# A fused linear-attention and feed-forward kernel: loads and output transfers moved to the SP queue, with a new order of the work

## The chip, the cores and the metric

The kernel runs on 1 core of one Trainium2 chip. The metric is the device time of the whole launch in microseconds (us), as the median of several runs. The engines are PE (TensorE, matrix products), DVE (VectorE), ACT (ScalarE), POOL (GpSimd) and SP (SyncE, which here only issues DMA transfers). Each runs its own list of instructions in order; a semaphore tells one engine that another, or a transfer, is done.

## What is computed

First a linear attention with a decaying state, for 4 sequences of 768 steps, 8 heads of 48 numbers. Then every one of the 3072 tokens (384 numbers) passes a feed-forward layer of 2048 hidden numbers whose activation is a rational function:

```python
for t in range(S):
    cur = np.einsum('bhd,bhe->bhde', u[None] * kt, vt)
    y[:, :, t] = np.einsum('bhd,bhde->bhe', rt, state + cur)
    state = w[None, :, :, None] * state + np.einsum('bhd,bhe->bhde', kt, vt)
...
h = x @ w_in
P = a[0] + a[1] * h + a[2] * h2 + a[3] * h3
Q = 1.0 + np.abs(b[0]) * np.abs(h) + np.abs(b[1]) * h2
g = P / (Q + 1e-06)
return (g @ w_out).astype(np.float32)
```

The weights w_in and w_out come as 8-byte numbers, and the kernel turns them into pairs of 4-byte ones itself.

## The kernel before

The attention is cut into 24 blocks of 128 steps (four sequences of six, `blk`), and two blocks make one tile of 256 tokens, 12 in all. The hidden numbers are worked in slices: a slice is one tile and up to four groups of 128 hidden numbers (the table `SL`, 50 slices, the first 47 of four groups).

- **A block** loads r, k and v (`att_load`, L445, three transfers of 192 KB: `rh`, `kn`, `vn`) and a copy of v with its halves exchanged (`att_v`, as a transfer L455 or as a copy L400). POOL scales k and makes the bonus term, PE transposes k and r (L494), forms the scores and the state (`akv`, L516 and L520) and the result (`y`, L564 and L566); DVE masks, adds and moves (L485, L507, L527, L541, L545, L577 or L580). PE turns the result (`x`, L590) and it is split into a high and a low part, `xthi` and `xtlo` (L400, L604).
- **A piece of weights** (28 of them, `swi` and `swo`) is loaded (`cv_load`, L370), handled by ACT (L375, L378), by DVE (L382, L385, with one of the PSUM buffers `pa0`, `pa1`, `h0`, `h1` in between), by POOL (L389), then split by ACT (L394) and POOL (L397).
- **A slice** is PE's first product (L615, 36 matmuls, into one of the two PSUM buffers `h0` and `h1`), then ACT: absolute value (L652), square (L661), square (L656), logarithm (L665), exponential (L669); DVE: L673, L678, L682, L686 and L691. The L691 is the last that reads the buffer `h`, so the slice after the next can begin its first product behind it. Then PE's second product (L619 to L621), and the result goes out by ACT or DVE (L738 to L742) and an output transfer of 192 KB (`put_dma`, L746).
- **A check of the inputs** (`pro_flag`, L327 to L344, some 15 tiny DVE instructions) runs once, somewhere among the weights.

Which engine does each step, in which order and in which buffer, stands in the string `ORDER`: a table of some 1,770 entries that a planner wrote. `Lk.5Slx2` is the load of k of block 5, issued by SP into buffer `lx2`; the capital letter is the engine (D, A, G, P, S for DVE, ACT, POOL, PE, SP). `cl` is the load of a piece of weights, `Lr`, `Lk`, `Lv`, `LV` are loads of a block, `od` is an output transfer, `f1` and `f2` are the two products, `ex` is L669, `lo` is L691, `warm` are matmuls on ones whose result is not used. The loop that reads the table:

```python
for task in ORDER.split():
    task, e, slot = re.fullmatch(r"(.+)([A-Z])((?:[a-z]+\d)*)", task).groups()
    name, *at_ = task.split(".")
    at_ = [int(x) for x in at_]
    here[:] = re.findall(r"[a-z]+\d", slot)
    FN[name](ENG[e], *at_)
```

A transfer waits, on the engine that issues it, for the readers of the buffer that it fills, and for an earlier transfer that used the same one of eight semaphores (`DMAHW0` to `DMAHW7` in the lists below). Nothing behind it on that engine starts before.

Of the kernel before, what the change touches and what calls it, by code (L numbers as in the profile page):

```python
# [49 lines left out]
pad.2G plGos0 pad.0G mskG Lr.0A warm.1P tr.0Ph0 wS Lr.1A pad.1G warm.3P tr.1Ppa0 cl_D ctrA pow.0D pow.2D inv.2Dta0 coefS betaA rxD  # L50
bet2A inv.3D inv.0D warm.4P turn.0.1Ph1 pow.1D pow.3D turn.2.1P turn.3.1P inv.1D warm.2P turn.1.1P cl.1S c0.1A Lk.0Slx0 ba.0Gm0
tre.0D tre.1D c2.1Dh0 sqD tab.1A sk.0G Lk.1Slx1 sk.1G Lv.0Sldv0 uwS warm.7P tk.0Ppa1 Lv.1Sldv1 tke.0A warm.3P akv.0Ppa0pa1 kvm.0A
LV.0.0Avx0 c3.1D ae.0.1.0D w128D ae.0.0.0D ae.0.1.1D bb.0G bs.0Ddt0 ae.0.0.1D Lk.2Slx2 tk.1Ph1 tke.1A warm.3P akv.1Ph0 cu.1A
LV.1.0Avx1 LV.0.1A warm.1P y.0Ph1 ae.1.0.0D kvx.0D cl.2S cu.2A c0.2A cl.0S c0.0A ba.1Gm1 bb.1G bs.1Ddt1 ae.1.1.0D c2.2Dpa0
ae.1.0.1D bv.0G sk.2G warm.3P tk.2Ppa1 tke.2A cr.1Gta1 c3.2D ye.0D Lr.2S warm.3P tr.2Ppa0 bv.1G ba.2Gm2 cr.2Gta2 c2.0Dpa1 kvm.1A
kvx.1D ae.1.1.1D LV.1.1A cl.8S c0.8A ch.1A warm.5P y.1Ph1 tre.2D c3.0D c2.8Dpa0 ye.1D bb.2G c3.8D Lv.2Sldv2 akv.2Ph0 ae.2.1.0D
cu.0A co.1G warm.1P x.0Ph1 cl.4S c0.4A c2.4Dpa1 bs.2Ddt0 xh.0Axt0 x.1Ppa0 xh.1A xl.0D cu.4A cr.0Gta3 ch.0A kvm.2A c3.4D xl.1D
Lr.3S Lk.3Slx0 warm.5P tr.3Ph1 tre.3D sk.3G tk.3Ppa1 ae.2.0.0D kvx.2D ae.2.0.1D ae.2.1.1D Lv.3Sldv3 ch.2A LV.3.0Avx2 tke.3A
LV.2.0Avx0 LV.2.1A LV.3.1A warm.3P akv.3Ppa0pa1 ae.3.1.0D ae.3.1.1D cl.9S c0.9A c2.9Dh1 kvm.3A kvx.3D c3.9D ae.3.0.0D ae.3.0.1D
co.0G co.2G f1.0.0Ph0 f1.0.1P f1.0.2P cl.6S Lk.4Slx1 c0.6A cu.9A cu.6A ba.3Gm3 bb.3G sk.4G bv.2G cl.5S c0.5A c2.6Dpa1 c2.5Dpa0  # L60
cu.5A cu.8A tk.4Ph1 tke.4A cl.3S c0.3A f1.0.3P z.0Ata4 c3.6D bs.3Ddt1 bv.3G c3.5D c2.3Dpa1 cr.5Gta5 y.2Ph1 ye.2D c3.3D cl.21S
# [4 lines left out]
cr.4Gta0 co.5G ca.2G c0.22A cu.12A ch.6A co.6G c0.13A cu.18A c0.12A ch.8A bs.4Ddt0 d.0D c2.7Dpa1 lo.0Dta5 c2.22Dpa0 c3.7D c3.22D
LV.4.1A ch.4A c2.12Dpa1 warm.19P f1.1.0Ph1 f1.1.1P f1.1.2P f1.1.3P z.1Ata4 warm.3P tk.5Ph0 tke.5A c0.16A c2.16Dpa0 ca.1G co.8G
bv.4G co.4G cr.7Gta3 c3.12D warm.3P tr.5Ph0 tre.5D c3.16D c2.13Dpa1 cu.21A cu.22A t.1Ata6 u3.1D f2.0.0P os.0.0Aos1 akv.5Ph0
ae.5.1.0D c3.13D ae.5.1.1D kvm.5D ae.5.0.0D kvx.5D ae.5.0.1D warm.2P f2.0.1P Lk.7Slx0 LV.5.1S cr.12Gta1 cr.11Gta0 ba.5Gm1 ch.11A
co.11G bb.5G bs.5Ddt1 cu.13A LV.11.0Avx2 Lr.6A cl.19S ch.12A q.1A ln.1A cl.25A y.4Ppa0pa1 ye.4D Lk.6Alx1 cl.15S Lr.7A cl.17S  # L70
cl.24S c0.10A c2.10Dpa0 warm.6P y.5Ph0 bv.5G ye.5D ex.1A hi.1Dta0 cr.21Gta2 sk.7G cr.9Gta5 warm.2P x.4Ppa1 xh.4Axt2 c0.19A warm.8P
x.5Ph0 xh.5A xl.5D xl.4D warm.26P f1.2.0Ph0 f1.2.1P f1.2.2P ch.21A cu.10A os.0.1Aos2 co.21G co.12G c0.25A cu.15A cr.13Gta2 ch.7A
cl.20A ch.9A co.9G ca.3G co.7G ch.13A c0.15A cl.14S f1.2.3P t.2Ata1 Lk.8Slx2 ba.6Gm2 co.13G bb.6G p.1D d.1D c2.19Dpa1 lo.1Dta4
c3.10D f2.1.0P f1.3.0Ph1 f1.3.1P f1.3.2P f1.3.3P flagD c2.15Dpa0 z.2Ata6 q.2A u3.2D ln.2A ex.2A cl.26S cu.16A c0.14A os.1.0Aos3
Lv.9Aldv3 z.3Ata5 t.3Ata3 q.3A cl.23A c3.15D c3.19D c2.25Dpa0 bs.6Ddt0 c3.25D hi.2Dta2 p.2D d.2D lo.2Dta6 u3.3D sk.6G tk.6Ppa1
f2.1.1P ba.7Gm3 ca.5G bb.7G cr.10Gta0 ch.10A tr.6Ppa0 tre.6D cr.22Gta4 ch.22A c0.20A c2.14Dpa0 bs.7Ddt1 c3.14D ln.3A ex.3A
hi.3Dta1 p.3D d.3D lo.3Dta5 Lv.7Sldv4 Lk.9Slx1 LV.7.0Svx1 LV.7.1S LV.6.0Svx0 c0.26A c0.23A cl.27S LV.6.1S co.10G ca.4G co.22G
# [843 lines left out]
```

## Time and profile before

| | |
|---|---|
| median of 3 runs | 552.5 us (551.88 to 552.65) |
| the profiled execution | 552.59 us |
| its span, first to last instruction | 550.9 us |
| PE busy | 522.2 us (95%) |
| DVE busy | 479.2 us (87%) |
| ACT busy | 349.3 us (63%) |
| POOL busy | 150.6 us (27%) |
| mean granted TensorE clock | 0.986 |
| read from memory, written | 27.87 MB, 4.72 MB |

A share of busy time is a mean over stages with different limits, so the stretches below are read one by one. "Idle before <-releaser" in a row is the time that the engine stood before the instruction, and what it waited for. A busy PE also holds the `warm` matmuls.

### The profile page before, as it was taken

To read this page: it belongs to the slowest core of one execution; us is meant where nothing else is said; L and a number is where in the kernel's file an instruction comes from. 1 tells how busy PE (TensorE), PEld (TensorE's weight loads), DVE (VectorE), ACT (ScalarE), POOL (GpSimd) and SP (SyncE) were. 2 spreads that over 40 slices of the span, in tenths; PEclk is the share of its full clock that TensorE was granted. 3 is DMA by queue.
4 is the path that set the end of the run, shared out by engine and by line. 5 is a ranking of instruction groups with operands and counts; after the bars stand their busy time and mean duration, and the time that the engine had idled before them with its cause. 6 is when DMAs were issued, how large, how long until landed. Compare 5 with 4: busy or idle time off the path is not lost.

```text
span 550.9 us, 14335 instructions
## 1 busy us (share of the span) xinstructions
PE 522.2 (95%) x6213; PEld 493.6 (90%) x6213; DVE 479.2 (87%) x648; ACT 349.3 (63%) x428; POOL 150.6 (27%) x167
## 2 busy tenths in 40 slices
PE   7895995999999999999999999999999999999994
...
DVE  6996999999899998988989988899698898887774
...
GB/s 160 247 288 285 152 120 107 33 16 29 68 15 2 2 56 76 21 59 52 40 46 80 61 61 30 1 30 23 41 34 15 15 15 2 31 15 15 1 29 65
DMA packets 88455, 33.60 MB, mean 61 GB/s; under 512 B 81600, under 2 KB 84800, under 8 KB 88384
## 3 DMA queue, kind: packets, MB, share of 16 engines
q1 hardware_dynamic: 60288, 21.13, 16.1%
...
q14 instruction: 20, 0.16, 0.1%
HBM read 27.87 MB, written 4.72 MB: 59 GB/s over the span
## 4 chain that ended last, share of the span: by engine, by line
PE 63%; DVE 9%; ACT 3%; issue 1%; ACTq 0%
PE h L615 27%; PE o L619 9%; PE o L621 9%; PE o L620 9%; PE akv L516 2%; DVE h L686 2%; DVE q L682 1%; DVE h L673 1%; PE y L566 1%; PE tk L494 1%; PE akv L520 1%; PE tr L494 1%; DVE g L678 1%; PE y L564 1%; PE x L590 1%
## 5 line engine op out<-in xcount | busy, mean ns | idle before, releaser
L615 PE MATMUL h<-xthi,wi 128*128 128x256 f32 x1152 | 220.7, 285 | 9.4 <-DVE sc L527 6.1
L615 PEld LDWEIGHTS h<-xthi,wi 128*128 128x128 f32 x1152 | 182.2, 189 | 12.7 <-ACT wo L394 6.6
L615 PE MATMUL h<-xtlo,wi 128*128 128x256 f32 x576 | 161.6, 281 | 0.1
L619 PE MATMUL o<-wo,g 128*128 128x384 f32 x384 | 133.0, 346 | 0.1
L620 PE MATMUL o<-wo,g 128*128 128x384 f32 x384 | 129.9, 338 | 0.0
L621 PE MATMUL o<-wo,l 128*128 128x384 f32 x380 | 128.7, 339 | 0.1
L615 PEld LDWEIGHTS h<-xtlo,wi 128*128 128x128 f32 x576 | 109.2, 190 | 0.2 <-DVE xtlo L604 0.2
L661 ACT ACTIVATE z<-h,off,root 128x1024 f32<-128x1024 f32 (+1 forms) x48 | 57.4, 1196 | 60.1 <-PE h L615 52.3
L678 DVE SCALAR_TENSOR_TENSOR g<-h,sig,z 128x1024 fp32r<-128x1024 f32 (+1 forms) x48 | 61.0, 1271 | 37.2 <-ACT z L669 37.0
L652 ACT ACTIVATE q<-h 128x1024 f32<-128x1024 f32 (+2 forms) x50 | 49.3, 987 | 45.2 <-PE h L615 40.0
L665 ACT ACTIVATE z<-q,sig 128x1024 f32<-128x1024 f32 (+1 forms) x48 | 54.9, 1143 | 36.4 <-DVE h L673 33.7
L619 PEld LDWEIGHTS o<-wo,g 128*128 128x128 f32 x384 | 72.8, 190 | 1.4 <-PE idle_bank L779 0.6
L620 PEld LDWEIGHTS o<-wo,g 128*128 128x128 f32 x384 | 72.8, 190 | 0.0
L621 PEld LDWEIGHTS o<-wo,l 128*128 128x128 f32 x380 | 72.0, 189 | 0.6 <-DVE l L691 0.5
L475 POOL TENSOR_TENSOR m<-rh,kn 128x384 f32<-128x384 f32 x23 | 25.5, 1108 | 162.5 <-PE x L590 67.9
L682 DVE SCALAR_TENSOR_TENSOR q<-q,sig,g 128x1024 f32<-128x1024 f32 (+2 forms) x50 | 64.7, 1294 | 1.7
L673 DVE SCALAR_TENSOR_TENSOR h<-z,sig,h 128x1024 f32<-128x1024 f32 (+1 forms) x48 | 61.1, 1272 | 4.3 <-ACT q L652 2.7
L686 DVE SCALAR_TENSOR_TENSOR h<-h,sig,q 128x1024 f32<-128x1024 f32 (+2 forms) x50 | 62.3, 1246 | 1.0
L656 ACT ACTIVATE q<-q,off,root 128x1024 f32<-128x1024 f32 (+2 forms) x50 | 60.4, 1209 | 0.8
L691 DVE TENSOR_TENSOR l<-h,z 128x1024 fp32r<-128x1024 f32 (+1 forms) x48 | 58.1, 1211 | 2.0
L669 ACT ACTIVATE z<-z 128x1024 f32<-128x1024 f32 (+1 forms) x48 | 50.5, 1052 | 6.6 <-DMA rh<-in_r_dram 5.2
L527 DVE TENSOR_TENSOR sc<-akv,mask 64x256 f32<-64x256 f32 x96 | 40.3, 420 | 6.1 <-PE akv L520 2.8
...
## 6 DMA issues: line engine op xcount, KB each, us to landing
...
out_dram<-os ACTq DMA_DIRECT2D x24, 192.0 KB, 2.0
vn<-in_v_dram SPq DMA_DIRECT2D x19, 192.0 KB, 4.5
kn<-in_k_dram SPq DMA_DIRECT2D x18, 192.0 KB, 3.6
rh<-in_r_dram ACTq DMA_DIRECT2D x12, 192.0 KB, 2.8
rh<-in_r_dram SPq DMA_DIRECT2D x12, 192.0 KB, 3.8
...
```

Of the source, the lines that this page charges most:

```text
L615: nc.tensor.matmul(o, wi_of(j, cc, part), x_[:, cc], start=(n == 0), stop=(n == 3 * NCC - 1))
L619: nc.tensor.matmul(o, hi, wo_of(j, HI), start=first, stop=False)
L620: nc.tensor.matmul(o, hi, wo_of(j, LO), start=False, stop=False)
L621: nc.tensor.matmul(o, lo, wo_of(j, HI), start=False, stop=last)
L656: nc.scalar.activation(g["q"], g["q"], AF.Square, scale=RB, bias=KB)
L661: nc.scalar.activation(g["t"], g["h"], AF.Square, scale=RA, bias=KA)
L665: nc.scalar.activation(g["z"], g["q"], AF.Ln, bias=QE)
L673: nc.vector.scalar_tensor_tensor(g["h"], g["t"], KAP, g["h"], op0=ALU.add, op1=ALU.mult)
L678: nc.vector.scalar_tensor_tensor(g["hi"], g["h"], c0, g["z"], op0=ALU.add, op1=ALU.mult)
L682: nc.vector.scalar_tensor_tensor(g["q"], g["q"], qe, g["hi"].bitcast(F32), op0=ALU.add, op1=ALU.mult)
L686: nc.vector.scalar_tensor_tensor(g["h"], g["h"], c0, g["q"], op0=ALU.add, op1=ALU.subtract)
L691: nc.vector.tensor_mul(g["lo"], g["h"], g["z"])
```

## The change

Only the string `ORDER` differs. Before, ACT issued 28 loads and all 24 output transfers besides its arithmetic; now it issues the first two loads of r and the last two output transfers, and SP all others. 26 loads and 22 output transfers so move from ACT's list to SP's. The order of all tasks was planned anew, with a planner that counts PE's instruction fetches as longer; a few tasks change engine (three `os` from DVE to ACT, one `xh`, one `tke`, one `sk`, one `ba` and one `bv` to DVE, and the like), and the `warm` matmuls go from 120 to 100. From the diff, two lines of before and two of the change, in which `cl.7A`, `cl.12A`, `cl.12S` and `Lv.5S` can be seen:

```diff
-x.2Ppa0 Lv.4Sldv4 cl.18S q.0A Lk.5Slx2 cl.22S xh.2Axt1 x.3Ppa1 xh.3A xl.2D c0.18A cr.3Gta0 ca.0G akv.4Ph1 ae.4.0.0D cl.7A ln.0A
-cl.12A ex.0A LV.4.0Avx1 xl.3D ae.4.1.0D kvm.4D c2.18Dpa0 ae.4.0.1D ba.4Gm0 cr.8Gta1 bb.4G cl.13S Lv.5Sldv0 Lv.11Sldv1 sk.5G
...
+tre.4D cl.12S c0.12A c2.12Dpa1 warm.1P y.3Ph1 ye.3D z.0Ata3 u3.0D warm.1P x.2Ppa0 xh.2Axt1 q.0A ln.0A c3.12D Lk.5Slx2 Lv.4Sldv4
...
+p.0D c2.16Dpa0 ch.5A bb.4G co.9G bb.5G cr.11Gta4 c0.13A LV.4.0Avx0 cl.22S Lv.5Sldv0 cl.10S cu.10A LV.5.0Avx1 LV.4.1A d.0D warm.1P
...
```

What the lists of the engines say of it, at three places.

**ACT, around the exponential of the first slice** (L669 into `z_769`, now `z_714`; `swi`, `swo` are pieces of weights, a DMA row is a transfer that ACT issues). Before:

```order
L375 ACTIVATE swo_778<-swo_778 128x384 [waits DMAHW7_49]
L370 DMA swi_0_832<-in_moe_w_in_dram 128x1024 [waits DMAHW2_49]
L665 ACTIVATE z_769<-q_678,sig 128x1024 [waits DVE_49,Activation_49]
L370 DMA swo_835<-in_moe_w_out_dram 128x768 [waits DMAHW6_49]
L669 ACTIVATE z_769<-z_769 128x1024 [waits Activation_49]
L400 COPY vx_838<-vn_776 64x192
```

Now:

```order
L656 ACTIVATE q_783<-q_783,off,root 128x1024 [waits Activation_49]
L665 ACTIVATE z_714<-q_783,sig 128x1024 [waits DVE_49,Activation_49]
L400 CAST xthi_791<-x_854 128x3x128 [waits PE_49]
L378 ACTIVATE swi_2_663<-swi_2_663 128x512
L669 ACTIVATE z_714<-z_714 128x1024 [waits Activation_49]
L394 CAST wo_868<-bwo_673 128x384 [waits Pool_49]
```

Two transfers, with their waits for a semaphore, are gone from ahead of the exponential; a copy and a conversion stand there instead.

**DVE, around L691 of the third slice** (`h_1252`, now `h_1249`; the L344 is the last instruction of the check of the inputs). Before:

```order
L344 TENSOR_REDUCE oks<-okw 128x1
L382 TENSOR_SCALAR c_1394<-swi_1_1142 128x512
L673 SCALAR_TENSOR_TENSOR h_1252<-z_1314,sig,h_1252 128x1024
L385 SCALAR_TENSOR_TENSOR swi_1_1142<-swi_1_1142,c_1394 128x512
L385 SCALAR_TENSOR_TENSOR swo_1096<-swo_1096,c_1324 128x384
L382 TENSOR_SCALAR c_1419<-swo_1102 128x384
L485 TENSOR_REDUCE dt_1421<-m_1318 128x8
L385 SCALAR_TENSOR_TENSOR swo_1102<-swo_1102,c_1419 128x384
L678 SCALAR_TENSOR_TENSOR g_1424<-h_1252,sig,z_1314 128x1024
L682 SCALAR_TENSOR_TENSOR q_1396<-q_1396,sig,g_1424 128x1024
L686 SCALAR_TENSOR_TENSOR h_1252<-h_1252,sig,q_1396 128x1024
L691 TENSOR_TENSOR l_1428<-h_1252,z_1314 128x1024
```

Now, ahead of the check:

```order
L382 TENSOR_SCALAR c_1245<-swo_1194 128x384
L382 TENSOR_SCALAR c_1247<-swo_907 128x384
L673 SCALAR_TENSOR_TENSOR h_1249<-z_1288,sig,h_1249 128x1024
L385 SCALAR_TENSOR_TENSOR swo_1194<-swo_1194,c_1245 128x384
L385 SCALAR_TENSOR_TENSOR swo_907<-swo_907,c_1247 128x384
L327 MEMSET lnb 128x1
```

and from its last instruction on:

```order
L344 TENSOR_REDUCE oks<-okw 128x1
L678 SCALAR_TENSOR_TENSOR g_1313<-h_1249,sig,z_1288 128x1024
L682 SCALAR_TENSOR_TENSOR q_1286<-q_1286,sig,g_1313 128x1024
L673 SCALAR_TENSOR_TENSOR h_1340<-z_1379,sig,h_1340 128x1024
L686 SCALAR_TENSOR_TENSOR h_1249<-h_1249,sig,q_1286 128x1024
L691 TENSOR_TENSOR l_1436<-h_1249,z_1288 128x1024
```

The L673 of the slice and the conversions now stand ahead of the check. Counted over the whole list, 126 tasks stand ahead of this L691 before and 124 now; ahead of the L691 of the seventh slice 178 stand in both, the same ones.

**SP, around the loads of weights between the first and the third slice** (`rh`, `kn`, `vn`, `vx` are loads of a block). Before:

```order
L445 DMA vn_875<-in_v_dram 128x8x48 [waits PE_49,DMAHW7_49,Activation_49,Pool_49]
L370 DMA swo_877<-in_moe_w_out_dram 128x768 [waits DMAHW0_49]
L455 DMA vx_879<-in_v_dram 64x4x48 [waits DMAHW1_49]
L445 DMA kn_1077<-in_k_dram 128x8x48 [waits DMAHW3_49]
L455 DMA vx_879<-in_v_dram 64x4x48 [waits DMAHW4_49]
L370 DMA swo_1096<-in_moe_w_out_dram 128x768 [waits DMAHW5_49]
```

Now:

```order
L445 DMA vn_1196<-in_v_dram 128x8x48 [waits DMAHW0_49]
L455 DMA vx_1198<-in_v_dram 64x4x48 [waits DMAHW1_49]
L370 DMA swo_1201<-in_moe_w_out_dram 128x768 [waits DMAHW2_49]
L445 DMA vn_1203<-in_v_dram 128x8x48 [waits PE_49,DMAHW3_49,Activation_49,Pool_49]
L370 DMA swo_1219<-in_moe_w_out_dram 128x768 [waits DMAHW4_49]
L370 DMA swo_1221<-in_moe_w_out_dram 128x768 [waits DMAHW5_49]
L370 DMA swi_1_1223<-in_moe_w_in_dram 128x1024 [waits DMAHW6_49]
L455 DMA vx_1226<-in_v_dram 64x4x48 [waits DMAHW7_49]
```

SP's list now holds every load of this stretch, and six loads of weights stand close behind `vn_1203`, the v of block 7, which waits for PE, ACT and POOL to be done with the buffer's earlier content.

## Rows read from the trace of the kernel before

**Rows 1.** The page: busy time of each engine, and the span in 40 slices.
```profile
PE 522.2 (95%) x6213; PEld 493.6 (90%) x6213; DVE 479.2 (87%) x648; ACT 349.3 (63%) x428; POOL 150.6 (27%) x167
PE   7895995999999999999999999999999999999994
DVE  6996999999899998988989988899698898887774
```
**Rows 2.** Busy time by stretch: us, engines with counts, granted clock, DMA share, GB/s.
```profile
0.00:10.00 10.00, 6.30 (x21) 3.71 (x22) 5.54 (x18) 4.05 (x14) 3.33 (x17) 1.00 0.79 160
10.00:46.70 36.70, 34.05 (x651) 23.39 (x650) 34.98 (x74) 25.39 (x49) 28.47 (x30) 1.00 0.92 252
46.70:51.80 5.10, 0.85 (x4) 0.20 (x2) 0.03 (x2) 1.09 (x2) 0.00 (x0) 0.87 1.15 294
51.80:80.00 28.20, 26.06 (x361) 23.32 (x362) 26.51 (x42) 25.05 (x44) 24.43 (x25) 0.90 0.59 173
51.80:60.00 8.20, 6.34 (x38) 6.12 (x39) 8.10 (x11) 7.22 (x16) 7.19 (x8) 0.67 0.93 329
80.00:100.00 20.00, 13.48 (x89) 13.06 (x88) 19.70 (x28) 12.31 (x15) 11.22 (x13) 0.83 0.36 86
100.00:136.60 36.60, 36.39 (x464) 34.87 (x465) 36.02 (x49) 32.75 (x46) 25.48 (x24) 1.00 0.09 18
136.60:545.00 408.40, 405.01 (x4643) 395.05 (x4635) 356.42 (x441) 248.70 (x261) 57.72 (x60) 1.00 0.15 33
```
**Rows 3.** Timeline of ACT, 43 to 52 us: start, us, instruction, idle before.
```profile
44.34 1.15 ACT L665 ACTIVATE z<-q,sig 128x1024 f32<-128x1024 f32 x1 [1.14 <-DMA swo<-in_moe_w_out_dram]
50.29 0.35 ACTq L370 DMA_DIRECT2D swo<-in_moe_w_out_dram  x1
50.69 1.06 ACT L669 ACTIVATE z<-z 128x1024 f32<-128x1024 f32 x1 [5.20 <-DMA rh<-in_r_dram]
```
**Rows 4.** Timelines of DVE, POOL and PE, the first instruction after the same stop.
```profile
51.77 1.28 DVE L678 SCALAR_TENSOR_TENSOR g<-h,sig,z 128x1024 fp32r<-128x1024 f32 x1 [5.07 <-ACT z L669]
52.73 1.00 POOL L397 TENSOR_TENSOR wo<-bwo,wo 128x384 fp32r<-128x384 f32 x1 [7.67 <-ACT wo L394]
53.66 0.55 PE L615 MATMUL h<-xthi,wi 128*128 128x256 f32 x1 [6.11 <-DVE sc L527]
```
**Rows 5.** Timelines of DVE and PE, where the fifth and the ninth slice begin.
```profile
95.37 1.23 DVE L691 TENSOR_TENSOR l<-h,z 128x1024 fp32r<-128x1024 f32 x1
96.74 0.36 PE L615 MATMUL h<-xthi,wi 128*128 128x256 f32 x1 [1.25 <-DVE l L691]
136.59 1.22 DVE L691 TENSOR_TENSOR l<-h,z 128x1024 fp32r<-128x1024 f32 x1
137.87 0.39 PE L615 MATMUL h<-xthi,wi 128*128 128x256 f32 x1 [0.86 <-DVE l L691]
```
**Rows 6.** Timelines of DVE, ACT and PE, the end of the check and after it.
```profile
87.15 0.69 DVE L382 TENSOR_SCALAR c<-swi 128x512 int32<-128x512 int32 x1
87.75 1.28 DVE L673 SCALAR_TENSOR_TENSOR h<-z,sig,h 128x1024 f32<-128x1024 f32 x1
89.13 1.15 ACT L665 ACTIVATE z<-q,sig 128x1024 f32<-128x1024 f32 x1 [7.29 <-DVE h L673]
90.24 1.08 PE L494 MATMUL tk<-ident,kh 128*128 128x128 f32 x4 [5.27 <-DVE swo L385]
```
**Rows 7.** Timeline of SP, 43 to 47 us: issue of the load that ACT waited for.
```profile
43.59 0.43 SPq L445 DMA_DIRECT2D rh<-in_r_dram  x1
```
**Rows 8.** The page, part 6: transfers that ACT issues; count, KB, median us to landing.
```profile
out_dram<-os ACTq DMA_DIRECT2D x24, 192.0 KB, 2.0
rh<-in_r_dram ACTq DMA_DIRECT2D x12, 192.0 KB, 2.8
```
**Rows 9.** Timeline of ACT, 68 to 69 us: two issues; and of PE, the only fetch gap.
```profile
68.53 0.39 ACTq L445 DMA_DIRECT2D kn<-in_k_dram  x1
20.44 0.59 PE L779 MATMUL idle_bank<-wones 128*128 128x512 bf16 x2 [1.37 <-issue]
```
**Rows 10.** Timelines of PE and ACT, the end of the program.
```profile
543.78 0.34 PE L621 MATMUL o<-wo,g 128*128 128x384 f32 x1
544.24 2.18 ACTq L746 DMA_DIRECT2D out_dram<-os  x2
```
**Rows 11.** Timeline of DVE and ACT, 69 to 72 us: block 4's result, a conversion.
```profile
69.63 0.62 DVE L580 TENSOR_TENSOR m<-y,m 128x192 f32<-128x192 f32 x2
71.86 0.58 ACT L375 ACTIVATE swo<-swo 128x384 f32<-128x384 f32 x1
```

More of the change, by code (lines that the diff above doesn't have):

```diff
@@ L49 @@
 ORDER = """
[L50 to L61, printed above, removed]
@@ L66 @@
[L66 to L77, printed above, removed]
@@ L162 @@
-od.10.1A q.47A ln.47A ex.47A hi.47D p.47D f1.48.0Ph0 f1.49.0P z.49A z.48A t.49A t.48A u3.48D q.48A ln.48A u3.49D q.49A d.47D
-flagmD lo.47D od.10.0A od.8.1A ex.48A hi.48D p.48D ln.49A ex.49A f2.46.1P f2.46.0P f2.47.0P hi.49D d.48D p.49D lo.48D d.49D
-f2.47.1P f2.48.1P f2.48.0P lo.49D f2.49.0P os.49.0Aos0 od.11.0A f2.49.1P os.49.1Dos4 od.11.1A
+Lr.1A pad.1G mskG plGos0 wS Lr.0A pad.0G pad.2G cl_D ctrA pow.0D inv.2Dta0 inv.3D coefS betaA rxD bet2A tr.1Ppa0 warm.3P tr.0Ppa1
+inv.0D warm.4P turn.0.1Ph0 turn.2.1P turn.3.1P pow.2D pow.1D pow.3D inv.1D warm.2P turn.1.1P tre.0D cl.1S Lk.1Slx0 ba.1Gm0 c0.1A
@@ new lines @@
+tre.1D c2.1Dh1 c3.1D sqD Lk.0Slx1 tab.1A sk.0G warm.6P tk.0Ph0 tke.0A cu.1A Lk.2Slx2 cl.4S Lv.0Sldv0 warm.3P akv.0Ph1 c0.4A w128D
+c2.4Dh0 c3.4D ae.0.1.0D ae.0.0.0D ae.0.1.1D ae.0.0.1D sk.1G tk.1Ppa1 ba.0Gm1 cr.1Gta1 sk.2G Lv.1Sldv1 uwS bb.1G LV.1.0Avx0 tke.1A
+warm.4P akv.1Ph0 ae.1.0.0D ae.1.1.0D ae.1.0.1D ae.1.1.1D ch.1A co.1G warm.1P tk.2Ppa0 LV.0.0Avx1 kvm.0A tke.2A kvx.0D bs.1Ddt0
+cl.2S cl.0S cu.2A LV.1.1A LV.0.1A warm.8P y.0Ph1 kvm.1A c0.2A kvx.1D bb.0G bs.0Ddt1 bv.0G c2.2Dh0 c0.0A c2.0Dpa1 Lr.2S ba.2Gm2
@@ new lines @@
+bv.1G warm.1P tr.2Ppa0 c3.2D ye.0D tre.2D c3.0D cr.2Gta2 warm.3P y.1Ph0 ye.1D x.0Ppa0 cl.8S Lk.3Slx0 cu.0A c0.8A c2.8Dpa1 c3.8D
+bb.2G cr.0Gta3 xh.0Axt0 warm.2P x.1Ph1 ch.2A xh.1A xl.1D Lv.2Sldv2 sk.3G Lr.3S ba.3Gm3 bs.2Ddt1 warm.2P tr.3Ph0 tre.3D xl.0D
+akv.2Ph1 ae.2.1.0D cl.3S ch.0A co.0G cu.8A c0.3A c2.3Dh0 ae.2.0.0D ae.2.0.1D c3.3D Lv.3Sldv3 tk.3Ppa1 tke.3A LV.3.0Avx2 cl.6S
+c0.6A cu.6A LV.3.1A warm.3P akv.3Ppa0pa1 kvm.3A kvm.2A cl.11S ae.3.1.0D ae.3.1.1D kvx.3D kvx.2D ae.3.0.0D ae.2.1.1D c2.6Dpa1
@@ new lines @@
+ae.3.0.1D co.2G warm.3P f1.0.0Ph0 Lk.4Slx1 sk.4G warm.2P tk.4Ph1 cu.11A cu.3A LV.2.0Avx1 c0.11A cu.4A bb.3G bs.3Ddt0 cl.5S c0.5A
+c2.5Dpa0 cr.8Gta4 bv.2G bv.3G cr.3Gta5 ca.0G c3.6D tke.4A c2.11Dh1 cl.9S c0.9A c2.9Dpa1 c3.11D cu.5A LV.2.1A ch.8A cr.6Gta6 ca.1G
+c3.9D c3.5D cr.5Gta0 cl.21S c0.21A ch.3A c2.21Dpa1 f1.0.1P f1.0.2P f1.0.3P t.0Ata1 Lr.4S y.2Ph1 ye.2D c3.21D warm.1P tr.4Ppa0
+tre.4D cl.12S c0.12A c2.12Dpa1 warm.1P y.3Ph1 ye.3D z.0Ata3 u3.0D warm.1P x.2Ppa0 xh.2Axt1 q.0A ln.0A c3.12D Lk.5Slx2 Lv.4Sldv4
@@ new lines @@
+warm.1P akv.4Ph1 ae.4.0.0D co.3G cr.4Gta2 ba.4Gm1 co.8G Lr.5S cl.13S ba.5Gm0 sk.5G kvm.4D ae.4.1.0D kvx.4D ae.4.0.1D warm.2P
+x.3Ppa1 xh.3A xl.3D xl.2D ae.4.1.1D cl.16S cu.9A ex.0A hi.0Dta5 ch.6A cu.21A cr.9Gta4 ch.9A c0.16A cu.13A warm.7P tr.5Ppa1 tre.5D
+p.0D c2.16Dpa0 ch.5A bb.4G co.9G bb.5G cr.11Gta4 c0.13A LV.4.0Avx0 cl.22S Lv.5Sldv0 cl.10S cu.10A LV.5.0Avx1 LV.4.1A d.0D warm.1P
+f1.1.0Ph1 f1.1.1P f1.1.2P tk.5Ppa1 f1.1.3P c3.16D lo.0Dta3 c0.22A LV.5.1A tke.5A c2.22Dpa0 cr.21Gta1 bs.4Ddt1 c2.13Dpa1 warm.6P
@@ new lines @@
+akv.5Ph0 ae.5.1.0D kvm.5D c3.13D ae.5.1.1D c3.22D ae.5.0.0D kvx.5D warm.10P y.4Ppa1pa0 cl.25S cl.7S Lr.6S cl.18S ae.5.0.1D y.5Ph0
+bs.5Ddt0 ch.11A cu.16A cu.7A co.11G bv.4G ye.4D x.4Ppa0 ch.21A ch.4A co.4G ca.2G co.6G co.5G f2.0.1P cu.22A c0.18A z.1Ata4 t.1Ata2
+u3.1D q.1A c2.18Dpa1 bv.5G Lv.9Sldv1 Lk.6Slx0 Lv.8Sldv2 Lr.8S cr.13Gta6 ba.6Gm2 co.21G ye.5D x.5Ph0 c0.25A c0.7A ln.1A xh.4Axt2
+xh.5A c3.18D c2.7Dpa1 c3.7D xl.5D xl.4D ex.1A hi.1Dta0 f2.0.0P cl.26S Lv.6Sldv3 LV.8.0Svx2 cu.26A cl.24S Lv.7Sldv4 cr.7Gta1 cu.24A
```

179 lines of the change are left out of this document (93 added, 86 removed).

## The prediction

> **What bounds the kernel now.** I read the page first [rows 1]. PE is busy 95% of the span, but its 40 slices are full only from the eighth on: the loss lies in the first 100 us and in the last few. So the table by stretch came next [rows 2]. From 136.6 to 545 us PE is busy 405.0 of 408.4 us while DVE has a tenth to spare: there PE's work alone sets the time. From 51.8 to 136.6 us it is the other way round. DVE is busy 26.51 + 19.70 + 36.02 = 82.2 of 84.8 us, while PE stands for 6.5 us between 80 and 100.
>
> The timelines at the seams show how one hands over to the other [rows 5]. The fifth slice begins on PE at 96.74 us, 1.25 us after PE ran dry, behind the DVE instruction L691 that frees its buffer. The ninth begins at 137.87 us behind another L691, which started at 136.59. Between the two, PE takes 41.13 us and DVE 41.22: both are full. So the path is DVE's list up to the L691 of the seventh slice, and from there PE's list to the end.
>
> Hence I counted DVE's idle time on that path. Busy time adds up to 5.54 + 34.98 + 0.03 + 26.51 + 19.70 + 36.02 = 122.8 of 136.6 us [rows 2], so it stands 13.8 us: 4.5 in the first 10 us, when nothing has arrived; 1.7 up to 46.7; **5.07 in a single stop at 46.7 to 51.8 us**; 1.7 up to 80; 0.9 after. The big stop is the thing to understand. DVE's L678 waited 5.07 us for ACT's exponential, POOL 7.67 us, PE 6.11 us [rows 4]. ACT itself stood 5.20 us ahead of that exponential [rows 3], and not for data that it uses: the row between is a transfer of w_out that ACT issues at 50.29 us, and the trace names the load of `rh` as what ended the wait. That load was issued by SP at 43.59 us [rows 7], so in this full stretch (294 GB/s [rows 2]) it took some 6.7 us. ACT stood only because it had to issue a transfer whose semaphore was still taken.
>
> **The change part by part.**
>
> *The loads leave ACT.* Ahead of the exponential ACT's list holds no transfer any more, so the 5.20 us there have no cause left, and DVE's stop behind it goes: **-5.07 us**. What would come late next is the data that ACT converts around there, which I price below. The smaller waits of ACT for a transfer that it issues itself, as the 1.14 us ahead of L665 [rows 3], go too, but DVE was full then (34.98 of 36.70 us, [rows 2]): nothing. The issues themselves took some 0.34 to 0.39 us each [rows 3, 9], and 48 of them are 16 to 19 us of ACT; ACT is busy 63% [rows 1] and is not on the path after 52 us: nothing, from 0 to perhaps 1 us of gain.
>
> *They join SP.* SP computes nothing, so its added 48 issues of 0.34 to 0.43 us [rows 3, 7] cost time only where a load behind them comes late. The 22 output transfers stand behind results that are long finished, so they hold nobody; the last two stay on ACT, where they took 2.18 us from 544.24 [rows 10], and the end of the program stays as it was. The 26 loads now share one list, and this has a price that the trace of before cannot show directly. From below it is nothing: from 10 to 46.7 us, when nearly every load was SP's, 252 GB/s were moved with the DMA engines busy 92% [rows 2]. From above: from 51.8 to 60 us, with loads from both engines, it was 329 GB/s. If SP alone cannot pass 252, then the 4.2 MB that 46.7 to 60 us moved (294 x 5.1 + 329 x 8.2) take 16.7 us instead of 13.3, and data is up to 3.4 us late. I take nothing, since the faster stretch carried more of the large loads of weights, and the fuller one more of the blocks. The Trainium skill (DMA: Bandwidth & Descriptors, "Issuing engines are not separate DMA queues") says that transfers from all engines end on the same 16 DMA engines and that a second issuing engine saves only the time of issuing. By that rule the term is nothing, by the rows taken at their face it is 3.4 us; no run here separates the two yet.
>
> *The new order.* Ahead of the L691 of the seventh slice stand the same 178 tasks of DVE, and ahead of the ninth slice's start the same tasks of PE, `warm` apart. So the work on the path has the same length before and after: 0. Up to the L691 of the third slice DVE's list is two tasks shorter, but a slice's L673 of 1.28 us replaces three short ones, some 0.6 us in all [rows 6]; as PE and DVE are both full between the fifth and the ninth slice, I give this nothing (0 to 0.6 us of gain). The check of the inputs no longer stands ahead of an L673 for which ACT waited 7.29 us, nor ahead of the conversion for which PE waited 5.27 us [rows 6]. These look large, yet DVE was busy 19.70 of 20 us then [rows 2]: they were the price of DVE's work, and where it stands changes nobody's sum. The granted clock of 0.67 and 0.83 in those stretches came after PE's stops and hit PE where DVE set the pace: nothing either way.
>
> *PE's fetches.* The only gap of PE that no engine explains before 100 us is 1.37 us at 20.44 us, ahead of `warm` matmuls that nobody waits for [rows 9]. A plan that allows for longer ones can win 0 to 1.37 us; I take 0. The 20 `warm` matmuls fewer filled waits: 0. The eight or so tasks that change engine weigh about 0.6 us each and shift ACT and DVE in both directions: 0.
>
> Sum: 552.59 - 5.07 = 547.5 us against the profiled execution's own time, which is 0.1 us from the median of 552.5. **Forecast: 547.5 us.** The lower bound closes the two stretches of 1.7 us in which DVE also waited: 547.5 - 3.4 = 544.1.
>
> **The rivals.**
>
> *A. SP's single list moves less.* The 3.4 us above come late on DVE: 550.9 us. For it speak 252 against 329 GB/s; against it the mix of loads, and that after 60 us the DMA engines are far from full (0.36 from 80 us on).
>
> *B. The wait moves from ACT's issue to ACT's data, and costs more.* `vn_1203` on SP waits until PE, ACT and POOL have finished with block 4, and `swo_1221`, for which ACT waits in its own order, stands two transfers behind. Before, block 4's result reached DVE at 69.63 us, and the conversion that corresponds ran on ACT at 71.86 us [rows 11]; its load did not stand behind that wait. If SP issues `swo_1221` only when ACT is about to reach it, ACT stands for a whole trip of a load, 6.7 us [rows 3, 7], and DVE behind it as before (5.07 of 5.20, so 6.5 us): 547.5 + 6.5 = **554.0 us, slower**. It decides from the point where the issue comes less than 6.7 us ahead of ACT's turn. Against it: in the new order block 4's result stands several places earlier on DVE, and the trips are shorter once the stretch is less full (median 2.8 us for `rh` from ACT, [rows 8]). The Trainium skill (DMA: Bandwidth & Descriptors, "Anatomy of one DMA") states that any wait for a semaphore is held by the issuing sequencer before dispatch; by that, a wait of `vn_1203` does hold all loads behind it, and rows 3 agree for ACT.
>
> *C. The stop is filled, not removed.* Were the data around 46.7 us late anyway, DVE would stop in another place for the same time: 552.5 us. For it speaks the DMA share of 0.92 up to 46.7 us and above 1 in the stop; against it that DVE's list up to there was full, so data was there. That the loads stay on ACT after all is excluded by the lists.
>
> **How the numbers follow.** Forecast (544 to 549.5) 0.52, A 0.14, B 0.23, C 0.11. About 0.2%, 1.1 us, is what a measurement of this kernel can tell from no change. The forecast and A are faster by more; C falls into the band, B is slower. I move 0.02 of A into the band: faster 0.64, same 0.13, slower 0.23. The range must reach over A and C to B, whose trip may be shorter or a little longer: 544.0 to 554.5; the likeliest case alone spans 544 to 549.5.
>
> **What would show it.** Right: no wait of ACT for a transfer ahead of the first exponential, no stop of DVE over 2 us between 10 and 90 us, the L691 of the seventh slice starting near 131.5 us and the ninth slice on PE near 132.8, and from there to the end the 413 us of before. Wrong: a stop of DVE behind an ACT that waits for `swo` or `swi` between 55 and 75 us (B), DVE idle spread over 46 to 65 us with a DMA rate near 252 GB/s (A), or a start near 132.8 us and yet no gain at the end, which would mean that PE's list behind it lost time of its own.

## The result, and the profile after

The changed kernel takes **543.99 us** (median of 4 runs, 542.77 to 545.53), the kernel before on the same chip 552.19 (550.26 to 552.65): a ratio of **0.9859**, 95% interval 0.9822 to 0.9897. By this ratio it is 7.8 us less (5.7 to 9.8), where 5.1 were forecast (547.5 us). The profiled execution took 545.53 us, with a span of 543.8.

The page first: busy times of the engines, the 40 slices of PE and DVE, and the queue of SP's transfers (q1) and of ACT's (q10).

```profile
PE 519.6 (96%) x6193; PEld 492.6 (91%) x6193; DVE 479.0 (88%) x647; ACT 348.8 (64%) x429; POOL 148.0 (27%) x165
PE   6788998999999999999999999999999999999996
DVE  6998999999989998989899989798787989887685
q1 hardware_dynamic: 86288, 31.86, 24.0%
q10 hardware_dynamic: 2368, 0.79, 0.6%
```

The totals are nearly those of [rows 1]; PE's row of digits differs in its first ten slices (the first 136 us) and in the last one. The table by stretch, with the same columns as [rows 2], its seam at the L691 of the seventh slice:

```profile
0.00:10.00 10.00, 5.73 (x19) 3.58 (x20) 5.45 (x18) 4.04 (x14) 3.53 (x17) 1.00 0.85 178
10.00:46.70 36.70, 29.87 (x582) 21.40 (x581) 34.72 (x68) 25.74 (x50) 30.31 (x33) 1.00 0.96 278
46.70:51.80 5.10, 4.79 (x64) 2.83 (x64) 3.33 (x8) 2.42 (x5) 2.30 (x3) 0.67 0.94 221
51.80:80.00 28.20, 26.31 (x369) 23.25 (x367) 27.79 (x43) 25.49 (x43) 22.68 (x23) 1.00 0.69 181
80.00:100.00 20.00, 17.29 (x114) 16.97 (x113) 19.73 (x34) 16.89 (x24) 9.13 (x11) 0.91 0.17 39
100.00:130.67 30.67, 30.63 (x432) 29.27 (x432) 29.89 (x42) 24.81 (x35) 22.50 (x22) 1.00 0.18 34
130.67:538.00 407.33, 404.14 (x4632) 394.86 (x4625) 357.46 (x439) 248.80 (x262) 57.51 (x60) 1.00 0.15 32
```

DVE's column adds up to 5.45 + 34.72 + 3.33 + 27.79 + 19.73 + 29.89 = 120.9 us of the 130.67 up to that L691. Before it was 122.8 of 136.6 [rows 2]. So DVE stands 9.8 us instead of 13.8, **4.0 us less**, and works **1.9 us less** for the same 178 tasks. The second part was not in the forecast at all. (How the gain divides differs from one execution to the next: in the profile of the changed kernel's second measurement DVE stands 3.8 us less and works 3.8 us less up to this L691, which starts at 128.98 us.) The timelines of DVE and PE at the seams of [rows 5]:

```profile
88.04 1.23 DVE L691 TENSOR_TENSOR l<-h,z 128x1024 fp32r<-128x1024 f32 x1
89.32 0.58 PE L615 MATMUL h<-xthi,wi 128*128 128x256 f32 x1 [2.71 <-DVE l L691]
130.67 1.23 DVE L691 TENSOR_TENSOR l<-h,z 128x1024 fp32r<-128x1024 f32 x1
131.95 0.39 PE L615 MATMUL h<-xthi,wi 128*128 128x256 f32 x1 [0.99 <-DVE l L691]
```

The ninth slice begins 5.9 us earlier, where 5.1 were forecast. But the fifth begins 7.4 us earlier, and the first L678, which was to gain 5.07 us, gains nothing. Timelines of ACT, PE and DVE there, to set against [rows 3, 4]:

```profile
45.90 1.15 ACT L665 ACTIVATE z<-q,sig 128x1024 f32<-128x1024 f32 x1
47.01 0.51 PE L516 MATMUL akv<-rt,kt 64*64 64x64 f32 x19 [2.04 <-issue]
48.12 0.42 DVE L527 TENSOR_TENSOR sc<-akv,mask 64x256 f32<-64x256 f32 x1 [2.00 <-PE akv L520]
49.73 0.48 ACT L400 CAST xthi<-x 128x384 fp32r<-128x384 f32 x1 [2.68 <-PE x L590]
50.67 1.05 ACT L669 ACTIVATE z<-z 128x1024 f32<-128x1024 f32 x1
51.82 1.28 DVE L678 SCALAR_TENSOR_TENSOR g<-h,sig,z 128x1024 fp32r<-128x1024 f32 x1
```

ACT waits for no transfer here any more. But in the new order the exponential stands behind a conversion whose data comes from PE, and PE stood 2.04 us in the middle of block 4's `akv` for nothing that an engine did: a gap of the kind of [rows 9], but now on the path. That it is a fetch of instructions is borne out by the transfers in the traces: the gap ends at 47.01 us, 1.35 us after a transfer of 16 KB on the instruction queue q8 was done (45.66 us), and the gap of [rows 9] ends 1.45 us after such a one. (Behind the gap PE's granted clock was 0.50, from 47.84 to 51.25 us; the one wait of DVE that the timeline lists in that time is 0.18 us, ahead of the L604 at 50.24.) Exponential and L678 start when they did before; in the second measurement's profile the gap is 1.76 us and the L678 starts at 50.67 us. The gain up to here is that DVE was not idle: up to 51.8 us it was busy 5.45 + 34.72 + 3.33 = 43.5 us, before 40.6.

Then the check of the inputs. Before, in the timelines of POOL and DVE (the rows ahead of those in [rows 6]):

```profile
82.33 1.02 POOL L480 TENSOR_TENSOR m<-m,ub 128x384 f32<-128x384 f32 x1
83.31 1.02 POOL L471 TENSOR_TENSOR kh<-kn,wkn 128x384 f32<-128x384 f32 x1
84.28 1.00 POOL L475 TENSOR_TENSOR m<-rh,kn 128x384 f32<-128x384 f32 x1
85.25 0.51 POOL L584 TENSOR_TENSOR vs<-vs,w 128x192 f32<-128x192 f32 x1
85.71 0.99 POOL L480 TENSOR_TENSOR m<-m,ub 128x384 f32<-128x384 f32 x1
...
79.11 0.06 DVE L327 MEMSET lnb<- 128x1 f32 x1
82.44 0.93 DVE L336 SCALAR_TENSOR_TENSOR ctmp<-ctmp,cabs 128x1 f32<-128x1 f32 x1
83.29 1.05 DVE L337 TENSOR_TENSOR ctmp<-cabs 128x1 f32<-128x1 f32 x1
84.38 0.93 DVE L338 TENSOR_TENSOR okw<-ctmp 128x1 f32<-128x1 f32 x1
85.23 0.54 DVE L339 SCALAR_TENSOR_TENSOR okw<-cabs 128x1 f32<-128x1 f32 x1
85.69 1.03 DVE L340 TENSOR_TENSOR ctmp<-cabs 128x1 f32<-128x1 f32 x1
86.75 0.16 DVE L341 SCALAR_TENSOR_TENSOR okw<-cabs,ctmp 128x1 f32<-128x1 f32 x1
```

and after:

```profile
80.72 1.02 POOL L471 TENSOR_TENSOR kh<-kn,wkn 128x384 f32<-128x384 f32 x1
...
80.07 1.68 DVE L331 TENSOR_TENSOR okw<-wraw,wcol 48x4 f32<-48x4 f32 x2
81.77 0.16 DVE L335 TENSOR_TENSOR ctmp<-cabs 128x1 f32<-128x1 f32 x1
81.97 0.16 DVE L336 SCALAR_TENSOR_TENSOR ctmp<-ctmp,cabs 128x1 f32<-128x1 f32 x1
83.02 1.28 DVE L678 SCALAR_TENSOR_TENSOR g<-h,sig,z 128x1024 fp32r<-128x1024 f32 x1
```

An instruction on one number per partition took about 1.0 us, each beside one product of POOL (0.54 beside POOL's 0.51), and 0.16 us from the moment POOL was done (86.70 us before, 81.74 after). The whole check took 8.0 us before (79.11 to 87.15) and 3.1 after (79.95 to 83.02): 5.0 us of DVE's busy time that the forecast had called neutral. Every wait ends with POOL: in the traces of both kernels (the changed one twice) and of runs 1 to 6 below, 42 of the check's instructions took over 0.3 us, none of them in run 4, and each ended 0.01 to 0.02 us after an instruction of POOL did.

### The profile page after: what moved, and what is told of

It reads as the page before. It is cut to its first block, busy times and chain, and to the rows that moved or that the text cites. A ratio compares the mean times of both kernels' runs of the same rounds, so it can differ in the third digit from the quotient of the medians.

```text
span 543.8 us, 14277 instructions
## 1 busy us (share of the span) xinstructions
PE 519.6 (96%) x6193; PEld 492.6 (91%) x6193; DVE 479.0 (88%) x647; ACT 348.8 (64%) x429; POOL 148.0 (27%) x165
## 4 chain that ended last, share of the span: by engine, by line
PE 62%; DVE 16%; ACT 4%; POOL 2%; issue 2%; DMA 1%; POOLq 0%; DVEq 0%; ACTq 0%
PE h L615 27%; PE o L619 9%; PE o L621 9%; PE o L620 9%; DVE q L682 3%; DVE h L686 3%; DVE g L678 2%; DVE l L691 2%; DVE h L673 2%; PE akv L516 1%; PE y L566 1%; PE y L564 1%; PE akv L520 1%; PE x L590 1%; PE tr L494 1%
## 5 line engine op out<-in xcount | busy, mean ns | idle before, releaser
L678 DVE SCALAR_TENSOR_TENSOR g<-h,sig,z 128x1024 fp32r<-128x1024 f32 (+1 forms) x48 | 61.0, 1271 | 35.7 <-ACT z L669 35.4
L682 DVE SCALAR_TENSOR_TENSOR q<-q,sig,g 128x1024 f32<-128x1024 f32 (+2 forms) x50 | 67.9, 1358 | 1.3
L673 DVE SCALAR_TENSOR_TENSOR h<-z,sig,h 128x1024 f32<-128x1024 f32 (+1 forms) x48 | 61.0, 1270 | 2.7 <-ACT q L652 1.4
L691 DVE TENSOR_TENSOR l<-h,z 128x1024 fp32r<-128x1024 f32 (+1 forms) x48 | 58.1, 1210 | 1.5
L489 POOL TENSOR_TENSOR m<-vn,dt 128x384 f32<-128x384 f32 x17 | 15.0, 886 | 136.7 <-DVE dt L485 136.7
L669 ACT ACTIVATE z<-z 128x1024 f32<-128x1024 f32 (+1 forms) x48 | 50.5, 1051 | 1.4
```

The lines of the kernel that those rows point to most:

```text
L673: nc.vector.scalar_tensor_tensor(g["h"], g["t"], KAP, g["h"], op0=ALU.add, op1=ALU.mult)
L678: nc.vector.scalar_tensor_tensor(g["hi"], g["h"], c0, g["z"], op0=ALU.add, op1=ALU.mult)
L682: nc.vector.scalar_tensor_tensor(g["q"], g["q"], qe, g["hi"].bitcast(F32), op0=ALU.add, op1=ALU.mult)
L691: nc.vector.tensor_mul(g["lo"], g["h"], g["z"])
```

## The experiments

Three theories. **L**: the gain is ACT's stop of 5.20 us, caused by a transfer that it had to issue. **F**: the gain is the check, which is long only beside POOL's work. **C**: the stop was only filled with another wait. All ratios are against the kernel before, run on the same chip, with 95% intervals. Of the long lines of `ORDER` the edits below show only the entries that change and one beside them.

| what runs | us | ratio |
|---|---|---|
| changed kernel, second time | 544.83 | 0.9855 (0.9829 to 0.9880) |
| old order, loads and outputs on SP | 545.36 | 0.9865 (0.9838 to 0.9891) |
| old order, `cl.12` alone on SP | 546.87 | 0.9913 (0.9891 to 0.9935) |
| old order, 22 outputs alone on SP | 551.47 | 0.9981 (0.9965 to 0.9998) |
| new order, 26 loads on ACT | 555.79 | 1.0064 (1.0040 to 1.0089) |
| old order, check late | 546.63 | 0.9885 (0.9861 to 0.9908) |
| new order, check late | 543.47 | 0.9822 (0.9797 to 0.9847) |
| old order, all on SP and check late | 541.03 | 0.9791 (0.9763 to 0.9820) |
| the same, second time | 540.43 | 0.9777 (0.9748 to 0.9806) |
| old order, `cl.12` on SP and check late | 541.79 | 0.9804 (0.9781 to 0.9828) |

**1. The engine that issues, without the new order.**

```diff
-cl.7A
-cl.12A
+cl.7S
+cl.12S
...
-od.1.1A
+od.1.1S
...
```

> The kernel before, with only the issuing engine changed: the 26 loads and the 22 output transfers that the change takes from ACT are issued by SP, at the same places of the old order. L (the gain of the change is ACT's 5.20 us stop): 552.2 - 5.1 = 547.1 us, DVE's 5.07 us stop ahead of the first L678 gone, the fifth slice about 5 us before 96.74 us on PE. C (the stop was only filled: something else makes DVE stand there for nearly as long): 551 to 552.5 us, another releaser for that stop. F (the gain is the check of the inputs, which runs faster where POOL is idle): 552 us, since the check stays at its place, 8.0 us long.

Measured 0.9865: all of what the change brings, within the intervals. The first L678 starts at 46.52 us, 5.25 earlier, and DVE is busy 5.00 of the 5.10 us in which it stood before. In the old order L holds and C does not. The new order adds nothing that can be measured: 0.9855 and 0.9859 with it. The gain passes L's 5.1 us by about 2. Up to the L691 of the seventh slice (128.93 us) DVE stands 4.3 us less and works 3.4 us less; 1.9 of this is the check, which took 6.3 us (72.67 to 78.97), as POOL's products fell otherwise beside it, and 1.6 are tiny instructions of the setup (L285, L290, L315).

**2. One transfer of the 48.**

```diff
-cl.12A ex.0A
+cl.12S ex.0A
```

> The kernel before with one entry changed: the load of the piece of w_out ahead of the first exponential (cl.12) is issued by SP, all the rest stays on ACT. L, if it is this one transfer: ACT's 5.20 us stop goes, the first L678 starts at 46 to 47 us instead of 51.8, and 553 - 5 to 7 = 546 to 548 us, nearly all of what the 48 gave (0.9865). If it is the crowd (any load on ACT meets a taken semaphore in the full stretch): another load of ACT stops it some microseconds later, and 551 to 553 us.

Measured 0.9913, that is 4.8 us (3.6 to 6.0), where the prediction had priced this stop at 5.07. The timelines of ACT and DVE (of the fastest of its six executions):

```profile
43.87 0.35 ACTq L370 DMA_DIRECT2D swi<-in_moe_w_in_dram  x1
44.32 1.15 ACT L665 ACTIVATE z<-q,sig 128x1024 f32<-128x1024 f32 x1 [1.40 <-DMA swo<-in_moe_w_out_dram]
45.51 1.06 ACT L669 ACTIVATE z<-z 128x1024 f32<-128x1024 f32 x1
46.60 1.28 DVE L678 SCALAR_TENSOR_TENSOR g<-h,sig,z 128x1024 fp32r<-128x1024 f32 x1 [0.16 <-ACT z L669]
```

The other issue, `cl.7` at 43.87, still holds ACT 1.40 us and costs DVE next to nothing: the step that gave it 0 was right. No later load on ACT takes the stop over: from 46.7 us to the L691 of the seventh slice DVE has no stop over 0.25 us. So it was this one place and not the crowd.

**3. The output transfers alone.**

```diff
-od.1.1A
+od.1.1S
...
```

> The kernel before with the 22 output transfers on SP and the 26 loads left on ACT. L: the stop ahead of the first exponential stays (5.1 us on DVE), so 552 to 553 us. If the issues of the output transfers on ACT (0.34 to 0.39 us each, some 8 us in all) were part of the gain: 549 to 551 us, with the part behind 138 us shorter than before.

Measured 0.9981, 1 us less (0.1 to 1.9). Not by the issues: from the start of the ninth slice to PE's end (135.2 to 541.7 us) the profile has 406.5 us, before 406.2 (137.9 to 544.1). In the profiled execution, the fastest of ten, the stop ahead of the first L678 was 1.42 us and not 5.07, with `cl.12` still on ACT. The edit did not do that: its first entry is the 797th of 1,771, behind the seam, and the order up to the stop is the one of before. In five profiles whose order is the same up to there the stop was 5.07, 4.55 (run 4), 4.20 and 5.25 (runs 5 and 6) and 1.42 us. So its length differs from one execution to the next. What sets it, and whether the 1 us is more than that, no run shows.

**4. The check alone, late.** It goes ahead of the L678 of slice 43, where DVE waits for ACT and POOL has no work.

```diff
-f1.3.3P flagD c2.15Dpa0
+f1.3.3P c2.15Dpa0
...
-od.9.0A hi.43Dta2
+od.9.0A flagD hi.43Dta2
```

> The kernel before, with only the check of the inputs moved on DVE from behind the fourth slice's first product to ahead of the L678 of slice 43, where DVE waits 2.4 us for ACT in every slice and POOL is idle. F: some 8.0 us leave DVE's full stretch and the check takes about 3 us in a gap: 552.2 - 8 = 544 to 545 us, the third slice's L691 at 87 to 88 us and the fifth slice on PE near 89. L: nothing changes, 552 us, since DVE's work was only at another place; if the check costs what its instructions take with POOL idle, 2.5 us, then 549.7 us.

Measured 0.9885, 6.4 us less (5.1 to 7.7), and not the 8; the L691 of the third slice starts at 89.7 us instead of 95.4. The check is gone from there, but that slice's L682 now takes 2.23 us instead of 1.28, beside POOL's products, and DVE stands 0.68 us for ACT ahead of its L673. Where it stands now, the check takes 1.77 us. Its first and last instruction, and the L678 behind it, which still waits for ACT:

```profile
494.74 0.06 DVE L327 MEMSET lnb<- 128x1 f32 x1
496.35 0.16 DVE L344 TENSOR_REDUCE oks<-okw 128x1 f32<-128x9 f32 x1
497.11 1.28 DVE L678 SCALAR_TENSOR_TENSOR g<-h,sig,z 128x1024 fp32r<-128x1024 f32 x1 [0.60 <-ACT z L669]
```

F holds in the old order. ACT's stop is still there (5.2 us), so the two causes are separate.

**5. Is it POOL?** The kernel of run 4, with ten products added on POOL beside the check; their result is not used.

```diff
+        spare = at.tile([P, H, D], F32, tag=here[0], name="spare")
+        for _ in range(10): nc.gpsimd.tensor_tensor(spare, ub, lnb[:, 0:1].unsqueeze(2).to_broadcast([P, H, D]), op=ALU.mult)
         for rows in HROWS:
```

> The kernel before with the check ahead of the L678 of slice 43, as in the run where it took 1.77 us, and with ten added products of 128x384 on POOL that start with it (their result is not used). F, if POOL's work is what lengthens the tiny DVE instructions: each one with two inputs from SBUF ends about when one of POOL's does, some 1.0 us apiece, and the check takes 7 to 9 us; the L678 behind it is late by as much, and the time is 4 to 6 us above that of the run without them. If the check was long before for another reason, as its place behind a large L691 or among the DMA traffic: about 2 us.

The check took 4.0 us. Timelines of POOL and DVE (the added lines shift the numbers by two; POOL's ten fill 9.85 us, and the second and third of them are shown by themselves):

```profile
494.71 9.85 POOL L331 TENSOR_TENSOR spare<-ub,lnb 128x384 f32<-128x384 f32 x10 [25.89 <-DVE okw L329]
495.62 0.83 POOL L331 TENSOR_TENSOR spare<-ub,lnb 128x384 f32<-128x384 f32 x1
496.53 0.83 POOL L331 TENSOR_TENSOR spare<-ub,lnb 128x384 f32<-128x384 f32 x1
...
495.77 0.70 DVE L338 SCALAR_TENSOR_TENSOR ctmp<-ctmp,cabs 128x1 f32<-128x1 f32 x1
496.39 0.15 DVE L339 TENSOR_TENSOR ctmp<-cabs 128x1 f32<-128x1 f32 x1
496.57 0.80 DVE L340 TENSOR_TENSOR okw<-ctmp 128x1 f32<-128x1 f32 x1
...
498.44 0.16 DVE L346 TENSOR_REDUCE oks<-okw 128x1 f32<-128x9 f32 x1
```

POOL's work alone more than doubles it, with no other change, but to 4.0 us and not to 7 to 9: about two instructions of DVE get through per product of POOL, where before it was one. The rows show what lets the second one through. The second product ends at 496.45 us and the third begins at 496.53: a gap of 0.08 us. The L339 begins at 496.39, ahead of the third product, and takes 0.15 us; the L340 begins at 496.57, after that product, and ends 0.01 us behind its end (497.37 and 497.36). The time, a single run of 547.95 us, is 1.3 above the median of run 4, not 4 to 6.

**6. With two full operands on POOL.**

```diff
-        for _ in range(10): nc.gpsimd.tensor_tensor(spare, ub, lnb[:, 0:1].unsqueeze(2).to_broadcast([P, H, D]), op=ALU.mult)
+        nc.gpsimd.tensor_tensor(spare, ub, lnb[:, 0:1].unsqueeze(2).to_broadcast([P, H, D]), op=ALU.mult)
+        for _ in range(9): nc.gpsimd.tensor_tensor(spare, ub, wkn, op=ALU.mult)
```

> As the run with ten added products of POOL beside the check (which then took 4.0 us instead of 1.77), but nine of the ten now read two full operands of 128x384, as POOL's work beside the check did in the kernel before. F with a wait for whole instructions of POOL: 6 to 8 us for the check, some 1.0 us for each tiny instruction. F with half the price: 4 us again, every second instruction 0.7 to 0.9 us, so that the 8.1 us of before would hold something more.

4.6 us (one run of 550.75 us; the first of the ten is as in run 5), and again every second instruction:

```profile
497.65 0.88 DVE L339 SCALAR_TENSOR_TENSOR ctmp<-ctmp,cabs 128x1 f32<-128x1 f32 x1
498.46 0.15 DVE L340 TENSOR_TENSOR ctmp<-cabs 128x1 f32<-128x1 f32 x1
498.64 0.99 DVE L341 TENSOR_TENSOR okw<-ctmp 128x1 f32<-128x1 f32 x1
```

So the operands' form is not the difference; the gap is. In runs 5 and 6 there are 0.08 us between the products beside the check, and every instruction of it that begins 0.03 to 0.14 us ahead of POOL's next product takes some 0.15 us. In the kernel before POOL's next product begins 0.04 to 0.06 us before the last one ends (82.33 + 1.02 = 83.35, the next at 83.31), so no gap is left. A DVE instruction that begins only 0.02 us ahead of POOL's next can wait all the same, as the L337 at 83.29 did, or get through, as two did in run 1 (75.66 and 76.64 us, 0.15 us each, POOL's next at 75.68 and 76.66). Why POOL leaves a gap in runs 5 and 6 was not tested; all ten products write one buffer there.

**7. The changed kernel with its check late.**

```diff
-c3.10D flagD os.0.0Aos2
+c3.10D os.0.0Aos2
...
-ex.43A hi.43Dta4
+ex.43A flagD hi.43Dta4
```

> The changed kernel with the check moved to ahead of the L678 of slice 43. F: the check took 3.1 us (79.95 to 83.0) there, which leave DVE's full stretch: 544.0 - 3.1 = 541 us. L: DVE's work only moves, 544 us.

0.9822, with an interval that reaches that of the changed kernel (0.9822 to 0.9897): between nothing and the 3.1 us. The trace, of the slowest of the five executions, says why it need not be all of it: DVE now stands 1.46 us for ACT's exponential ahead of the L678 at 83.0 us, where the check had filled the time. It also stands 2.93 us behind a fetch gap of PE that was 2.31 us this time, which lies ahead of all that the edit moved.

**8. The changed kernel with the 26 loads back on ACT.**

```diff
-cl.12S c0.12A
+cl.12A c0.12A
...
```

> The changed kernel with the same 26 loads back on ACT, at the places of the new order; the output transfers stay on SP. If the order by itself gives nothing: about 550 to 552 us, with a wait of ACT for a transfer that it issues between 40 and 90 us. If the new order by itself gives what its check of the inputs saves (5 us): 547 us. If the order alone avoids the stop, wherever the loads are issued: 544 to 545 us.

1.0064, slower than the old order. Issue and use of one piece of w_out on ACT:

```profile
39.58 0.35 ACTq L370 DMA_DIRECT2D swo<-in_moe_w_out_dram  x1
47.36 0.55 ACT L375 ACTIVATE swo<-swo 128x384 f32<-128x384 f32 x1 [5.61 <-DMA swo<-in_moe_w_out_dram]
```

The new order writes a load a few places ahead of its use. That is enough for SP, which computes nothing and runs ahead, and too late for ACT. It is rival B's wait, on the other engine: none of the three outcomes that were expected. Order and issuing engine belong together here, so this run does not give the order's worth by itself; run 1 does.

**9. Both causes together.** Loads and outputs on SP and the check late, in the old order:

> The kernel before with both edits: loads and output transfers on SP, and the check ahead of the L678 of slice 43. If L and F are both true and add: 552.2 - 5.1 - 8 = 539 us. F with C: 544 to 545 us, as with the check alone. L alone: 547 us.

Measured 0.9791, less of a gain than the sum of runs 1 and 4 (0.9865 + 0.9885 - 1 = 0.975) and than the 539 us that were expected: the check had lost 1.9 us in run 1 already, and without it DVE stands 1.82 us for ACT ahead of the L673 at 75.07 us. And with only two entries of the order changed:

```diff
-cl.12A ex.0A
+cl.12S ex.0A
...
-od.9.0A hi.43Dta2
+od.9.0A flagD hi.43Dta2
```

> The kernel before with two entries of the order changed: the load cl.12 issued by SP (alone 0.9913) and the check of the inputs ahead of the L678 of slice 43 (alone 0.9885). L and F as two separate causes on DVE's list: 0.9913 + 0.9885 - 1 = 0.980, some 541.9 us, less than the changed kernel. If the two overlap, as with all loads on SP (0.9791 where the sum is 0.975): 0.983 to 0.985, about 544 us.

Measured 0.9804, 541.8 us, as the sum of the single gains (0.9913 + 0.9885 - 1 = 0.9798) says. The L691 of the seventh slice starts at 124.05 us and PE's ninth slice at 125.33, against 136.59 and 137.87 [rows 5]. On the same chip, beside it:

> The changed kernel itself once more, to stand on the same chip beside the two that the experiments point to: 0.986 of the time before, 544 to 545 us.

> The old order with loads and output transfers on SP and the check ahead of the L678 of slice 43, once more beside the changed kernel: 0.979, 541 us, 3 us below the changed kernel. If the two were only measured on different chips: within 1 us of it.

0.9855 and 0.9777: the old order with both edits is 4.4 us below the changed kernel (544.83 and 540.43), and the two intervals do not touch.

## Why the prediction was right, and where it was not

- **"ACT's 5.20 us there have no cause left, and DVE's stop behind it goes: -5.07".** Right in kind and size: 4.8 us for the one transfer. The 5.07 is the length in one execution; in five it lay between 1.42 and 5.25 (run 3). All loads on SP gave 7.5, more than the stop, since DVE also worked 3.4 us less in that profile, 1.9 of it the check.
- **The same step, "What would come late next ... price below", and "PE's fetches ... I take 0".** This failed. In the new order the first L678 gains nothing (51.82 against 51.77; 1.1 us in the second profile): PE's fetch gap of 2.04 us lies on the path at 47 us, and the stop became work done earlier (3.0 us) and a shorter stop (2.00, in the second profile 2.13, which is at the prediction's own mark of 2 us for a stop that should not be there). A fetch gap was priced by where it stood before, not by what the new order puts behind it. And it was not free before: PE runs its list in order, and behind the `warm` matmuls of [rows 9] stands a transpose for which ACT waited, and DVE 0.64 us behind ACT (the rows are at the end of this document). Rival C happened in part.
- **"Where it stands changes nobody's sum" (the check), and "the work on the path has the same length before and after: 0".** This is the step that was wrong. The same 178 tasks took 1.9 us less: the check 5.0 less, the seven L682 1.9 more (1.79 against 1.53 us on the average), four tiny instructions of the setup (L279, L280, L284, L315) 1.8 more, the rest some 0.6 less. In the second profile the check took 2.8 us, and the whole work was 3.8 less. The rows for it were in the trace of before: seven of the check's 15 tiny instructions at 0.9 to 1.2 us apiece, called the price of DVE's work.
- **"They join SP: 0, from 0 to 3.4".** Right: SP alone moved 278 GB/s from 10 to 46.7 us, above the 252 that rival A took for a limit. The Trainium skill (DMA: Bandwidth & Descriptors, "Issuing engines are not separate DMA queues") says that transfers started by several engines run on the same 16 DMA engines and that this saves only the time of starting them. The trace agrees: one issuing engine was enough for these 278 GB/s.
- **Rival B** did not occur: no wait of ACT for `swo` or `swi` between 55 and 75 us.
- **The end.** From the L691 at the seam to PE's last product it is 408.1 us, before 407.5; the rest of the 7.1 us between the two profiled executions is the tail behind PE, 5.0 against 6.8 us, which lies between 5.1 and 6.5 in the other runs and is 5.5 in the second profile of the changed kernel. No run shows that the change shortened it.

So the cause that was named is real, but that the number came out near for this kernel is partly luck: a stop that did not go as a whole, and a check that became shorter, nearly offset each other. The seams of the prediction's list (131.5 and 132.8 us forecast, 130.67 and 131.95 found) could not tell. Only the first L678 could.
